# Layout of the phase products between two passes, and the order of blocks and weight loads

## The chip, the core and the metric

The kernel runs on one core of one Trainium2 chip. The metric is the device time of one execution in microseconds (us). The core's engines are PE (TensorE, matrix products; PEld is its weight load), DVE (VectorE), ACT (ScalarE), POOL (GpSimd) and SP (SyncE). SP, ACT and POOL issue DMA transfers; the transfers themselves run on 16 DMA engines. In the profile q0 is the queue of the DMAs that POOL issues, q1 that of SP, q10 that of ACT.

## The reference

The input x has 8 batches of 5696 tokens with 128 channels. The first half is a long convolution over the tokens with a filter h; its result is the x of the second half:

```python
Yf = np.fft.rfft(x, n=L, axis=1) * np.fft.rfft(h, n=L, axis=0)[None]
x = np.fft.irfft(Yf, n=L, axis=1)[:, :S, :]
theta = x @ w_theta
zr, zi = x * np.cos(theta), x * np.sin(theta)
y = np.einsum('ts,bsd->btd', w_tok_r, zr) + np.einsum('ts,bsd->btd', w_tok_i, zi)
u = x + y
out = u + np.maximum(u @ w_ch, 0.0)
```

The two products with the 5696 x 5696 matrices w_tok_r and w_tok_i (the token mixing) take most of the time.

## The kernel before, in words

*Convolution (0 to about 383 us).* The FFT is done as matrix products in 8 groups (two batches by half the channels). The result yt goes to a DRAM scratch. In the last group the phase steps of the first four batches are woven in between: `phase_step` (L736) turns a tile of 128 tokens by PE, takes sine and cosine on ACT and multiplies on DVE, which gives the two products zr and zi in one SBUF tile zz, [128, 2, 512] in bf16. It also copies the tile to a y buffer (L754; six of them in a ring) and stores it (L756).

*z's scratch and the operand blocks.* The products are the right-hand operands of the token mixing. Tokens are cut into 22 blocks a pass (p = 0, 1 are two parts of the contraction; 11 blocks j, each of four pieces i of 64 tokens). The columns are 1024, cut in two halves q (four batches each); z counts the two products. For half q = 0 of all tokens, and for what is not needed at once, `phases_b` (L550) stores 64 tokens at a time into the DRAM scratch z_hbm (L620). In SBUF a block j is a tile b{j} of 7 x 1024 columns: four operands (q, z), each with two neighbouring tokens r side by side, and three slots for sums. DVE makes five sums a block (`sum_ops`, L833; in the profile L835), since the mixing is done by seven products instead of eight (Strassen), except in the first stretches, which use the plain eight. `load_b_half` (L824) loads half q = 0 of blocks 0 to 8 for pass 0 from the scratch, by two DMAs on POOL (L829), one for each z. Half q = 1 of these blocks comes straight from zz by the home stores (L616), r = 0 on SP and r = 1 on POOL. `load_b` (L814) loads a whole block: blocks 9 and 10 of pass 0 on SP and all 11 of pass 1 on ACT, by two DMAs each (L817).

*Pass order.* The second set of 22 phase steps is woven into the first products of pass 0 (stretch i = 1, L1210): after every second product one step runs. Then pass 0 and pass 1 go through 23 token tiles each; a tile takes two chunks (6 and 5 blocks), a chunk two stretches of up to 3 blocks. L1290 is the matmul of the seven-product stretches, L1210 that of the plain ones, L1178 that of the last 64 tokens. The rest of the phase work (`bg_phase`, L911) runs beside pass 0 and stores by L623.

*W loads.* The f32 matrices come by `load_w` (L673): one load is four DMAs of 32 partitions on POOL (L680), cast to bf16, into a ring of six slots. `pump` (L652) issues loads while a slot's former chunk has been read and while their number is below ring["upto"], which the code raises by hand: six times in the last group of the convolution (`with_load`, L768), twice in stretch i = 1 (L1224), and then to the end. A chunk needs four loads. DVE transposes them (L894) before PE uses them.

*What sets the order.* Each engine runs its instructions in the program's order; a scheduler places them, but DVE's order around the start of each pass is written by hand. `tc.issue_after(...)` holds an instruction behind another on its queue. A tile that takes the place of older ones in SBUF waits until those are done with. The blocks' tiles (pool bpool_e) lie where the convolution had its own, among them yt.

Of the kernel before, what the change touches and what calls it, by code (L numbers as in the profile page):

```python
# [11 lines left out]
BF16 = mybir.dt.bfloat16  # L12
# [10 lines left out]
def kernel(  # L23
# [10 lines left out]
    nc = tc.nc  # L34
# [6 lines left out]
    BD = B * D  # L41
    HALF_PI = math.pi / 2.0

    z_hbm_h = nc.dram_tensor("z_hbm", (2, 11, 2, 2, 4, 64, BD // 2), BF16, kind="Internal")
    zl_hbm_h = nc.dram_tensor("zl_hbm", (2, 64, BD), BF16, kind="Internal")
    y2_hbm_h = nc.dram_tensor("y2_hbm", (NT, P, B, D), BF16, kind="Internal")
    wl_hbm_h = nc.dram_tensor("wl_hbm", (P, NT, P), BF16, kind="Internal")
# [502 lines left out]
    def phases_b(ti, y_ap, b0, nb, yT, sb, th_pool, th_tag, zi_eng, turns=None, tags=("red", "mag"), m=P,  # L550
                 theta_ps=None, copy=None, home={}):
        n = nb * D
        if theta_ps is None:
            theta_ps = th_pool.tile([P, n], F32, tag=th_tag, name="theta_ps")
        theta_ps = theta_ps[:m]
        y_ap = y_ap[:m]
        if tags is None:
            sin_, cos_ = (sb.tile([P, n], F16, tag=t, name=t)[:m] for t in ("sin", "cos"))
        else:
            red, mag = (sb.tile([P, n], F32, tag=t, name=t_)[:m] for t, t_ in zip(tags, ("red", "mag")))  # L560
            sin_, cos_ = (z.bitcast(F16)[:, :n] for z in (red, mag))
        if turns is None:
            for b in range(nb):
                nc.tensor.matmul(theta_ps[:, b * D:(b + 1) * D], yT[:, b, :],  # L564
                                 w_theta_sb, start=True, stop=True)
            nc.scalar.activation(red, theta_ps, AF.Identity, bias=magic[:m])  # L566
            nc.scalar.activation(mag, theta_ps, AF.Copy)
            nc.vector.scalar_tensor_tensor(red, red, MAGIC, mag,
                                           op0=ALU.subtract, op1=ALU.subtract)
            r = red  # L570
        else:
            mag = theta_ps
            ones, plus, minus, w_neg = turns
            for q in range(0, nb, 4):
                bank = theta_ps[:, q * D:(q + 4) * D]
                nc.tensor.matmul(bank, ones, plus, start=True, stop=False)
                for b in range(q, q + 4):
                    nc.tensor.matmul(theta_ps[:, b * D:(b + 1) * D], yT[:, b, :],
                                     w_theta_sb, start=False, stop=False)
                nc.tensor.matmul(bank, ones, minus, start=False, stop=False)  # L580
                for b in range(q, q + 4):
                    nc.tensor.matmul(theta_ps[:, b * D:(b + 1) * D], yT[:, b, :],
                                     w_neg, start=False, stop=(b == q + 3))
            r = theta_ps
        if copy is not None:
            copy()
        if turns is None:
            nc.scalar.activation(mag, r, AF.Abs)
        nc.scalar.activation(sin_, r, AF.Sin, bias=zero_b[:m], scale=-TWO_PI)
# [12 lines left out]
        zi_eng.tensor_mul(zi, sin_, yflat)  # L602
        nc.vector.tensor_mul(zr, cos_, yflat)
        cols = slice(b0 * D, b0 * D + n)
        q_ = b0 // 4
        for e in range((m + 63) // 64):
            rows = slice(e * 64, e * 64 + 64)
            if ti * P >= 2 * H:
                for r, z in enumerate((zr, zi)):
                    nc.sync.dma_start(zl_hbm[r, :, cols], z)  # L610
                continue
            p_, blk = divmod(2 * ti + e, 4 * NJ)
            i, j = divmod(blk, NJ)
            if tags is None and j in home:
                for r in range(2):
                    (nc.gpsimd if r else nc.sync).dma_start(  # L616
                        home[j][32 * i:32 * i + 32, :4096].rearrange("p (z q r n) -> p z q r n", z=2, q=2, r=2)[:, :, q_, r],
                        zz[e * 64 + r:e * 64 + 64:2])
            elif tags is None:
                nc.sync.dma_start(z_hbm[p_, j, q_, :, i].rearrange("z t n -> t z n"), zz[rows])  # L620
            else:
                for r, z in enumerate((zr, zi)):
                    nc.sync.dma_start(z_hbm[p_, j, q_, r, i], z[rows])  # L623

    CHUNKS = [(j0, min(CJ, NJ - j0)) for j0 in range(0, NJ, CJ)]
    pairs = (list(range(21)) + [None, 21], [0, None] + list(range(1, 22)))
# [149 lines left out]
    for g, (bp, dh) in enumerate(groups):  # L776
        st = {}
        last = g + 1 == len(groups)
        a_, load_, b_ = fronts.pop(g + 1) if g + 1 in fronts else front(g + 1)
        if last:  # L780
            for _ in range(3):
                steps0.pop(0)()
        now = ([with_load(steps0.pop(0), n < 6) for n in range(9)] if last else [], 0.0, 0.88)
        c_ = stage_c(st, last)
        if g == 0:
            ec = []
            swap_rows()
            now = ([lambda: ec.append(e_table(1)), lambda: ec.pop()(), lambda: ec.append(e_table(2)), lambda: ec.pop()(),
                    e_minus],
                   -0.1, 0.6)  # L790
        woven((c_, 0.06 if a_ else 0.0, 1.0), (a_, 0.0, 0.88), now, load_, (load_x(g + 2, st), 0.1, 1.02))
        if g == 0:
            ordered.close()
        if g + 2 == len(groups):
            xin.close()
            open_phases()
            load_ya0()
        now = [steps0.pop(0) for _ in range(5)] if last else []
        woven((b_, 0.0, 0.8), (stage_d(st, bp, dh, load_ya1 if last else None), 0.08 if b_ else 0.0, 1.1 if b_ else 1.0), now)
# [6 lines left out]
    bts_of = {0: [], 1: []}  # L806

    def tile_b(p, j, pool):
        t_ = ring["all"][:, WB:WB + BT] if j == 0 else pool.tile([P, BT], BF16, tag=f"b{j}", name=f"b{j}")
        bt = [t_[:, k * 1024:(k + 1) * 1024].rearrange("p (r n) -> p r n", r=2) for k in range(7)]  # L810
        bts_of[p].append(bt)
        return t_

    def load_b(p, j, pool, eng=nc.scalar):  # L814
        t_ = tile_b(p, j, pool)
        for z in range(2):
            sides["late"] = eng.dma_start(  # L817
                t_[:, z * 2048:(z + 1) * 2048].rearrange("p (q n) -> p q n", q=2),
                z_hbm[p, j, :, z].rearrange("q i (s r) n -> (i s) q (r n)", r=2))

    def home_pool(j):
        return bpe[0] if j < 7 else bpe[1] if j < NE else bp

    def load_b_half(j):  # L824

        t_ = home_of[j] = tile_b(0, j, home_pool(j))
        for z in range(2):
            with tc.issue_after(sides["row"]) if j else ExitStack():
                d_ = nc.gpsimd.dma_start(t_[:, z * 2048:z * 2048 + 1024],  # L829
                                         z_hbm[0, j, 0, z].rearrange("i (s r) n -> (i s) (r n)", r=2)).ins  # L830
            sides["row"] = d_ if j else sides["row"]

    def sum_ops(bt):  # L833
        b11, b12, b21, b22 = (bt[q] for q in (M2, M6, M7, M5))
# [8 lines left out]
    def sum_some(n):  # L843

        for o in [o for o in owed if o[1] <= 2 or done["used"] > o[0]][:n]:
            owed.remove(o)
            o[2]()

    for j in range(7):
        load_b_half(j)  # L850
    for step in steps0:
# [266 lines left out]
    for i, (k, p, tt, j0, s0, nj) in enumerate(stretches):  # L1118
# [97 lines left out]
        if i == 1:  # L1216
            for q, (h, s) in enumerate(((0, 0), (0, 1), (1, 0), (1, 1))):
                for n in range(4):
                    for j in range(TJ):
                        product((held, a)[s], s * TJ + j, j, n, (h,))  # L1220
                        if (n * TJ + j) % 2:
                            next_steps(1)
                    if n % 2 and q == 1:
                        ring["upto"] += 1  # L1224
                        pump()
                    if q == 3 and n == 0:
                        nxt = prepare(2)
            ring["upto"] = len(queue)
            pump()
            continue  # L1230
# [122 lines left out]
```

## Time and profile before

| what | value |
|---|---|
| median of 3 runs | 2037.92 us (2035.97 to 2045.31) |
| the profiled execution | 2040.29 us |
| its span, first to last instruction | 2038.5 us |
| mean granted PE clock | 0.987 |
| PE busy, 0 to 100 / 350 to 400 / 400 to 450 / 450 to 500 / 700 to 900 us | 74.4 / 37.1 / 47.4 / 45.2 / 198.9 us |
| PE busy, 1200 to 1300 us | 93.9 us |
| DMA queues: packets, MB, share of 16 engines | q0 322368, 157.47, 60.6%; q1 181792, 163.03, 27.3%; q10 5984, 11.54, 1.6% |
| z store (L620), 52 of 128 KB | 5.1 us to landing |
| home stores (L616), 32 on SP, 32 on POOL into b, 64 KB | 4.8 and 4.0 us |
| half block load (L829), 16 of 256 KB | 6.1 us |
| block load of pass 1 (L817 on ACT), 20 of 512 KB | 13.2 us |

How to read it: the span is the time between the first and the last instruction of one execution. A row of the timeline gives the start, the length, the engine, the line of the code, the operation, the tile written and read, and in brackets how long the engine stood idle before it and what ended that. The time to landing of a DMA runs from its issue to its completion. A wait is put down to what came last by the profile, which is inferred.

### The profile page before, as it was taken

Reading aid. Unit: us, or ns where it says so; the run is one execution under the profiler, and the core shown is the slowest. Engines: PE = TensorE matmul, PEld = TensorE weight load, DVE = VectorE, ACT = ScalarE, POOL = GpSimd, SP = SyncE. Lnnn points to the kernel's source line nnn. Section 1 sums busy time; section 2 is a strip of 40 time slices with the busy share of each in tenths; the row PEclk is TensorE's granted clock in tenths of the full one; section 3 lists DMA queues with packets and bytes.
Section 4 is the critical chain, followed back from the end, with each engine's and each line's share of the span. In section 5 each row is a group of like instructions: output and inputs, shape, how many; then the busy total and the mean of one; then the engine's idle time right before and its main releaser. Section 6 shows DMA issues by size and latency. Waiting matters only on the chain.

```text
span 2038.5 us, 42418 instructions
## 1 busy us (share of the span) xinstructions
PE 1944.0 (95%) x16121; PEld 1077.9 (53%) x16297; DVE 1539.8 (76%) x2817; ACT 638.9 (31%) x936; POOL 966.7 (47%) x1769
## 2 busy tenths in 40 slices
PE   7789898799999999999999998999999999999998
PEld 5688887654444444444444443444444444444444
DVE  8877877557778787887867668768677786777767
ACT  6788787762233323332300000111111111111111
POOL 8334213284353545454566454553545445354450
PEclk9999999899999999999999999999999999999999
DMA  9999988899798989999999798896978879788793
GB/s 155 163 173 145 161 164 231 244 261 178 157 180 173 174 173 162 181 173 181 165 173 152 122 247 206 137 154 126 153 136 141 151 126 155 130 151 142 134 157 84
DMA packets 510349, 334.77 MB, mean 164 GB/s; under 512 B 186631, under 2 KB 463111, under 8 KB 510055
## 3 DMA queue, kind: packets, MB, share of 16 engines
q0 software_dynamic: 322368, 157.47, 60.6%
q1 hardware_dynamic: 181792, 163.03, 27.3%
q10 hardware_dynamic: 5984, 11.54, 1.6%
q8 instruction: 128, 2.10, 0.4%
q14 instruction: 77, 0.63, 0.1%
HBM read 374.82 MB, written 95.24 MB: 231 GB/s over the span
## 4 chain that ended last, share of the span: by engine, by line
PE 66%; DMA 3%; DVE 3%; issue 1%; POOL 0%; ACT 0%; DVEq 0%
PE m L1290 61%; DMA ring<-in_moe_w_tok_i_dram 3%; DVE c L1297 1%; PE utp L974 1%; PE v L981 1%; PE m L1294 1%; DVE wt L894 1%; DMA ring<-in_moe_w_tok_r_dram 1%; PE theta_ps L564 0%; DVE b L835 0%; PE tpz L922 0%; PE m L1178 0%; POOL ring L680 0%; ACT ub L971 0%; DVE c L983 0%
## 5 line engine op out<-in xcount | busy, mean ns | idle before, releaser
L680 POOL DMA_DIRECT2D ring<-in_moe_w_tok_i_dram x720 | 388.6, 545 | 663.0 <-DVE wt L894 583.8
L680 POOL DMA_DIRECT2D ring<-in_moe_w_tok_r_dram x720 | 387.2, 546 | 130.2 <-DVE wt L894 70.9
L894 DVE STREAM_TRANSPOSE wt<-ring 128x384 f32<-128x384 f32 (+2 forms) x720 | 359.9, 525 | 115.6 <-PE m L1290 81.3
L1290 PE MATMUL m<-b,wt 128*128 128x512 bf16 x1604 | 384.8, 379 | 3.8 <-DVE wt L894 1.7
L1290 PEld LDWEIGHTS <-wt 128*128 128x128 bf16 x1804 | 176.0, 98 | 215.4 <-DVE wt L894 3.9
L1297 DVE TENSOR_TENSOR c<-c,m 128x512 f32<-128x512 f32 x412 | 265.9, 671 | 0.4 <-PE m L1290 0.4
L976 ACT ACTIVATE ring<-utp 128x512 bf16<-128x512 bf16 x85 | 50.7, 597 | 577.5 <-PE utp L974 577.5
L453 PE MATMUL ps<-r_u,uv_t 128*128 128x128 f16 x1024 | 117.3, 220 | 5.4 <-DVE g__1416 L460 2.0
L1210 PE MATMUL m<-b,wt 128*128 128x512 bf16 x471 | 113.0, 387 | 8.8 <-DMA b<-z_hbm 4.8
L971 ACT ACTIVATE ub<-c 128x512 bf16<-128x512 f32 x88 | 55.1, 628 | 201.0 <-DVE c L1253 118.6
L454 PE MATMUL ps<-r_v,uv_t 128*128 128x100 f16 x1024 | 115.3, 209 | 0.1
L153 POOL DMA_DIRECT2D x<-in_x_dram x128 | 99.5, 783 | 20.4 <-POOL x L151 14.9
L454 PEld LDWEIGHTS <-uv_t 128*128 128x128 f16 x1024 | 100.8, 99 | 5.9 <-issue 4.9
L433 DVE TENSOR_TENSOR uv_t<-xs,hs 128x2048 f16<-128x2048 f16 x77 | 91.5, 1223 | 16.3 <-DMA hs<-hf_hbm 9.2
L453 PEld LDWEIGHTS <-uv_t 128*128 128x128 f16 x1024 | 100.9, 98 | 2.3 <-DVE uv_t L438 2.1
L431 ACT ACTIVATE xs<-ps 128x1024 f16<-128x1024 f32 x96 | 90.8, 972 | 30.1 <-PE ps L270 14.3
L1210 PEld LDWEIGHTS <-wt 128*128 128x128 bf16 x528 | 51.5, 100 | 71.0 <-issue 12.6
L566 ACT ACTIVATE red<-theta_ps,magic 128x512 f32<-128x512 f32 (+1 forms) x46 | 31.6, 687 | 155.6 <-PE theta_ps L564 86.2
L270 PEld LDWEIGHTS <-w_t 64*128 64x128 f16 x3240 | 56.3, 98 | 31.0 <-issue 22.7
L924 ACT ACTIVATE ring<-tpz 128x512 bf16<-128x512 bf16 (+1 forms) x46 | 27.5, 597 | 134.0 <-PE tpz L922 120.2
L250 PE MATMUL ps<-f_t,x 89*128 89x180 f16 x512 | 62.0, 250 | 2.2 <-DVE a L257 1.8
L983 DVE SCALAR_TENSOR_TENSOR c<-v,c 128x512 f32<-128x512 f32 x88 | 60.1, 684 | 4.8 <-PE v L981 4.5
(2925 smaller groups left out, 3733.9 us busy)
## 6 DMA issues: line engine op xcount, KB each, us to landing
ring<-in_moe_w_tok_r_dram POOLq DMA_DIRECT2D x352, 96.0 KB, 4.4
ring<-in_moe_w_tok_i_dram POOLq DMA_DIRECT2D x352, 96.0 KB, 5.0
ring<-in_moe_w_tok_r_dram POOLq DMA_DIRECT2D x352, 80.0 KB, 4.6
ring<-in_moe_w_tok_i_dram POOLq DMA_DIRECT2D x352, 80.0 KB, 3.9
cp_hbm<-c SPq DMA_DIRECT2D x88, 256.0 KB, 2.5
c<-cp_hbm SPq DMA_DIRECT2D x88, 256.0 KB, 4.5
out_dram<-c SPq DMA_DIRECT2D x88, 256.0 KB, 4.7
hs<-hf_hbm SPq DMA_DIRECT2D x77, 256.0 KB, 3.5
```

What stands on the lines that cost most here:

```text
L153: nc.gpsimd.dma_start(x16[p0:p1, e, n0:n0 + 16, :HD], bass.AP(tensor=src.tensor, offset=src.offset + (p0 * N2 + n0) * D + dh * HD, ap=[[N2 ...
L250: nc.tensor.matmul(ps[:, i // 2, (i % 2) * 2 * K1:(i % 2 + 1) * 2 * K1], lhs(q + i), f1_t[:NB], start=True, stop=True)
L431: nc.scalar.activation(xs[:, :, :, :ck], ps, AF.Copy)
L433: nc.vector.tensor_tensor(uv[:, :, :, c0:c0 + ck], xs.rearrange("p e d k -> p e (d k)").unsqueeze(1).to_broadcast([P, 2, 2, HD * CK]), hv. ...
L453: nc.tensor.matmul(o, u_t[:, at:at + P], r_u, start=True, stop=False)
L454: nc.tensor.matmul(o[:, 2 * NP:], v_t[:, at:at + P], r_v, start=False, stop=True)
L680: nc.gpsimd.dma_start(wb[32 * i:32 * i + 32, :ng, :nj * 64], bass.AP(tensor=a.tensor, offset=a.offset + row0 * S + p * H + i * QR + j0 * 6 ...
L894: nc.vector.transpose(wt.rearrange("p j t r -> p (j t r)").bitcast(F32).rearrange("p (j g t) -> p g j t", j=TJ, g=4)[:, :ng, :nj], wb[:, : ...
L983: nc.vector.scalar_tensor_tensor(c[:m], v[:m], 0.0, c[:m], op0=ALU.max, op1=ALU.add)
L1210: nc.tensor.matmul(ms[n // 2 * 2 + h], a[n][:, j, :, r], bts_of[p][jj][n % 2 * 2 + h][:, r, :], start=(n % 2 == 0 and jj == 0 and r == 0), ...
L1290: nc.tensor.matmul(ms[q], a[q][:, j, :, r], bts[jj][q][:, r, :], start=(jj == 0 and r == 0), stop=(jj == NJ - 1 and r == 1 and q not in left))
L1297: nc.vector.tensor_tensor(c, z, ms[q], op=op)
```

## The change

1. The scratch z_hbm is laid out as (pass, block, q, piece, token, z, column) instead of (pass, block, q, z, piece, token, column): the two products of a token stand side by side. A z store from zz (L620) then has rows of 2 KB instead of 1 KB; the background stores (L623) keep rows of 1 KB, with 2 KB between them in DRAM.
2. In SBUF the four operands of a block are laid out as (q, r, z, column) instead of (z, q, r, column). A home store has one row of 2 KB a partition instead of two of 1 KB. A whole block is loaded by one DMA for each q, with rows of 4 KB, instead of one for each z with two rows of 2 KB. A half block is loaded by one DMA with rows of 4 KB instead of two with rows of 2 KB. An operand is no longer 1024 columns in a run but two runs of 512; matmuls read one run at a time, as before.
3. The tiles of blocks 0 and 6 to 1 are allocated ahead of the loads, in that order, so that they lie in SBUF the other way round. The loads of blocks 1 and 2 are no longer held behind sides["row"] (the DMAs of ya1); those from block 3 on are.
4. Of the six W loads in the last group of the convolution four stay in stage c and two move into stage d. In stretch i = 1 ring["upto"] is raised in two quarters instead of one, so four loads are issued there ahead of the rest instead of two.

```diff
-    z_hbm_h = nc.dram_tensor("z_hbm", (2, 11, 2, 2, 4, 64, BD // 2), BF16, kind="Internal")
+    z_hbm_h = nc.dram_tensor("z_hbm", (2, 11, 2, 4, 64, 2, BD // 2), BF16, kind="Internal")
...
                 for r in range(2):
+                    at = 2048 * q_ + 1024 * r
                     (nc.gpsimd if r else nc.sync).dma_start(
-                        home[j][32 * i:32 * i + 32, :4096].rearrange("p (z q r n) -> p z q r n", z=2, q=2, r=2)[:, :, q_, r],
+                        home[j][32 * i:32 * i + 32, at:at + 1024].rearrange("p (z n) -> p z n", z=2),
                         zz[e * 64 + r:e * 64 + 64:2])
             elif tags is None:
-                nc.sync.dma_start(z_hbm[p_, j, q_, :, i].rearrange("z t n -> t z n"), zz[rows])
+                nc.sync.dma_start(z_hbm[p_, j, q_, i], zz[rows])
             else:
                 for r, z in enumerate((zr, zi)):
-                    nc.sync.dma_start(z_hbm[p_, j, q_, r, i], z[rows])
+                    nc.sync.dma_start(z_hbm[p_, j, q_, i, :, r], z[rows])
...
-        now = ([with_load(steps0.pop(0), n < 6) for n in range(9)] if last else [], 0.0, 0.88)
+        now = ([with_load(steps0.pop(0), n < 4) for n in range(9)] if last else [], 0.0, 0.88)
...
-        now = [steps0.pop(0) for _ in range(5)] if last else []
+        now = [with_load(steps0.pop(0), n < 2) for n in range(5)] if last else []
...
-        bt = [t_[:, k * 1024:(k + 1) * 1024].rearrange("p (r n) -> p r n", r=2) for k in range(7)]
-        bts_of[p].append(bt)
+        raw = t_[:, :4096].rearrange("p (q r z n) -> p q z r n", q=2, r=2, z=2)
+        bt = [raw[:, k % 2, k // 2] if k < 4 else
+              t_[:, k * 1024:(k + 1) * 1024].rearrange("p (r n) -> p r n", r=2) for k in range(7)]
+        bts_of[p][j] = bt
...
-        for z in range(2):
+        for q in range(2):
             sides["late"] = eng.dma_start(
-                t_[:, z * 2048:(z + 1) * 2048].rearrange("p (q n) -> p q n", q=2),
-                z_hbm[p, j, :, z].rearrange("q i (s r) n -> (i s) q (r n)", r=2))
+                t_[:, q * 2048:(q + 1) * 2048],
+                z_hbm[p, j, q].rearrange("i (s r) z n -> (i s) (r z n)", r=2))
...
-        t_ = home_of[j] = tile_b(0, j, home_pool(j))
-        for z in range(2):
-            with tc.issue_after(sides["row"]) if j else ExitStack():
-                d_ = nc.gpsimd.dma_start(t_[:, z * 2048:z * 2048 + 1024],
-                                         z_hbm[0, j, 0, z].rearrange("i (s r) n -> (i s) (r n)", r=2)).ins
-            sides["row"] = d_ if j else sides["row"]
+        if j not in home_of:
+            home_of[j] = tile_b(0, j, home_pool(j))
+        with tc.issue_after(sides["row"]) if j > 2 else ExitStack():
+            d_ = nc.gpsimd.dma_start(home_of[j][:, :2048],
+                                     z_hbm[0, j, 0].rearrange("i (s r) z n -> (i s) (r z n)", r=2)).ins
+        sides["row"] = d_ if j > 2 else sides["row"]
...
+    for j in (0, 6, 5, 4, 3, 2, 1):
+        home_of[j] = tile_b(0, j, home_pool(j))
     for j in range(7):
         load_b_half(j)
...
-                    if n % 2 and q == 1:
+                    if n % 2 and q in (1, 2):
                         ring["upto"] += 1
                         pump()
```

More of the change, by code (lines that the diff above doesn't have):

```diff
@@ L805 @@
     bpe = [ctx.enter_context(tc.tile_pool(name="bpool_e", bufs=1, side="right", reuse_waits="tile"))]
-    bts_of = {0: [], 1: []}
+    bts_of = {0: {}, 1: {}}
     def tile_b(p, j, pool):
         t_ = ring["all"][:, WB:WB + BT] if j == 0 else pool.tile([P, BT], BF16, tag=f"b{j}", name=f"b{j}")
-        bt = [t_[:, k * 1024:(k + 1) * 1024].rearrange("p (r n) -> p r n", r=2) for k in range(7)]
-        bts_of[p].append(bt)
+        raw = t_[:, :4096].rearrange("p (q r z n) -> p q z r n", q=2, r=2, z=2)
+        bt = [raw[:, k % 2, k // 2] if k < 4 else
+              t_[:, k * 1024:(k + 1) * 1024].rearrange("p (r n) -> p r n", r=2) for k in range(7)]
+        bts_of[p][j] = bt
         return t_
```

## The prediction

> **What bounds the kernel now.** I read the page's first two parts, then PE's waits by stage, the chain, the timeline where PE waits, and the DMA queues by stretch.
>
> ```profile
> span 2038.5 us, 42418 instructions
> PE 1944.0 (95%) x16121; PEld 1077.9 (53%) x16297; DVE 1539.8 (76%) x2817; ACT 638.9 (31%) x936; POOL 966.7 (47%) x1769
> ...
> PE 66%; DMA 3%; DVE 3%; issue 1%; POOL 0%; ACT 0%; DVEq 0%
> ```
>
> PE is busy 95%, and from 520 us on it hardly waits (4 us of waits up to 1100, none over 0.2 us between 1300 and 2000). No matmul is added or removed, so only PE's idle time can change, and it lies in three places that the change touches: the phase stage (340 to 440), the first chunks of pass 0 (440 to 470), and the start of pass 1 (1180 to 1260). The first two, from the timeline (start, length, engine, line; in brackets the idle time before it and what ended it):
>
> ```profile
> 350.64 0.69 ACT L589 ACTIVATE sin<-ps,zero_b 128x512 f16<-128x512 f32 x1 [1.95 <-DVE ring L754]
> 358.79 0.42 DVE L754 COPY ring<-ps 128x512 bf16<-128x512 bf16 x1 [2.26 <-DMA y_hbm<-ring]
> 394.82 4.84 POOL L829 DMA_DIRECT2D b<-z_hbm  x9 [8.72 <-DMA y_hbm<-ring]
> 398.62 0.92 PE L1210 MATMUL m<-b,wt 128*128 128x512 bf16 x2 [3.01 <-DMA b<-z_hbm]
> 401.71 0.69 ACT L589 ACTIVATE sin<-theta_ps,zero_b 128x512 f16<-128x512 f32 x1 [4.23 <-PE theta_ps L582]
> 448.40 1.07 POOL L616 DMA_DIRECT2D b<-zz  x2
> 449.46 1.13 POOL L680 DMA_DIRECT2D ring<-in_moe_w_tok_r_dram  x2
> 454.53 5.77 PE L1210 MATMUL m<-b,wt 128*128 128x512 bf16 x25 [1.39 <-DMA b<-zz]
> 463.50 1.83 PE L1210 MATMUL m<-ring,wt 128*128 128x512 bf16 x4 [3.20 <-DVE wt L894]
> ```
>
> See: ACT paces the phase steps (0.69 + 0.59 + 0.69 = 1.97 us a step); POOL's queue stands 8.72 us before block b1 is loaded; POOL issues its last home store (zz into b) at 449, and W loads 8 and 9 come only behind it. The start of pass 1 shows in the queues between 1210 and 1215 us (packets, MB, share of 16 engines):
>
> ```profile
> q10 hardware_dynamic: 570, 1.10, 64.3%
> q0 software_dynamic: 576, 0.39, 50.6%
> ```
>
> q10 carries the block loads of pass 1 (L817), q0 the W loads. Their packets go one for one: 443 to 443 (1192-1196), 564 to 560 (1200-1205), 575 to 576, 537 to 540 (1220-1225). So how much W gets is set by how long a packet of z is.
>
> **The change, part by part.**
>
> *z stores (L620) and home stores (L616).* As many DMAs; a z store has 64 rows of 2 KB for 128 of 1 KB, a home store 32 for 64. Issue costs stay: SP takes 0.59 us for a z store of 128 rows and 0.53 to 0.59 for L623's 64, POOL 0.54 whatever the shape. What can gain is landing. In the phase steps DVE's L754 waits for a y buffer, that is for the y store six steps earlier, which stands on SP among z stores: 1.46, 0.89 and 2.26 us of DVE, which give ACT 1.95, 1.32 and 1.45 us (4.7). With packets served in turn, half as many packets land sooner. The bounds are 0 and 4.7, with nothing lost, as bytes and DMAs stay; no row shows 2 KB stores from 64 partitions. I take -2, z stores being two of the three DMAs of a step. The background stores (L623) keep 64 rows of 1 KB and now step over 2 KB in DRAM; PE does not wait for them: 0.
>
> *Blocks in reverse order, b1 and b2 not held to the ya1 DMA, one load per half block (L829).* In the changed program b1's load no longer waits for the four DMAs that read yt (issued 383.98 to 386.1; the stores land after 8.0 us); b5's does. So b1 issues at 386.1 instead of 394.8, but behind yt's 1.4 MB in the same queue, whose packets run until about 393: 0.53 MB per 2 us there puts b1 at about 396 instead of 398.5. ACT's 4.23 us stall shrinks by 2.5 (bounds 1 and 4). POOL also issues 9 DMAs fewer (9 x 0.54 = 4.9 us), 7 of them where POOL now idles.
>
> *W loads.* Of loads 4 and 5 only the last DMA each (of four) moves, from 356.6 and 362.7 into stage d; W is not needed before 440: 0. Loads 8 and 9 (8 DMAs) move ahead of the last home stores. PE's 3.20 us at 463.5 goes; what is late next is block b10, whose SP load (455.05) waits for the home stores: I keep -2.7. The price is POOL's: from load 6 to the last home store it issued 39 DMAs in 24.2 us (0.62 each), now 47, so 29.2. It starts when step 10's products are ready, 2.5 + 2 us earlier for the parts above, and no longer lags (y store 0 went out at 403.88 with its data ready at 394.7). Before, load 6 went at 425.2; now about 419, less the 2: end at 446 to 448 instead of 449.5. Behind POOL's queue wait the last home stores, for them the sums of block 8 and PE's second half of blocks 6 to 8. So of the 4.5 us gained above PE keeps only what POOL lets through: -3.5 in all at 454.5 (bounds 0 and -6), the -2 and the -2.5 included. The y-slot stall on DVE (2.19 us at 439.96, then PE 2.04) goes into the same wait.
>
> *Sums (L835).* 110 of 128x1024 now read and write 512-element runs with gaps, at 684 ns before. Nearest row: L433, three-level operands, 128x2048 in 1222 ns, so 0.60 ns an element against 0.67. Cost 0; the upper bound is a rival below.
>
> *Pass 1 loads (L817).* 22 DMAs of 512 KB, rows of 4 KB for 2 KB. PE's waits for late blocks (1.08 + 0.72 us at 1248 and 1251) go: -1.8. Against that stands W. A pair of packets took 16 x 5 / 573 = 140 ns of an engine; by bytes read (1.93 KB of z, about 1.3 KB of f32 W) a pair with 3.86 KB takes 223. A W load came every 5.2 us in this stretch (POOL's issues, which wait for landings), so 8.1 us while z runs. The fifth one after 1190.5, W22 of the first chunk of pass 1, landed at about 1218.1 and PE needs it transposed at 1223.2, 4.5 us of slack. At 8.1 it is 10 us late. Bounds: 0 (a 4 KB row takes two turns, and the ratio stays) and +10; the nearest row is yt's, whose 5.6 KB rows show as single packets (66 of 0.32 MB at 388 to 390), so nearer the upper end. Less a part: z now outruns PE's release of blocks (b3 at about 1200, b6 at 1209) and leaves W gaps. I take +6.
>
> [...]
>
> **Sum.** -3.5 - 2.7 - 1.8 + 6 = -2.0 us. The profiled execution took 2040.3 (span 2038.5); that gives 2038.3. The median of the runs shown is 2037.9, 2.4 below that execution, so 2036 on its scale. Bounds: all gains (-6, -3.2, -1.8) and no starvation -11; no gain and all loss +10.
>
> **Rivals.**
> 1. *Faster, about 2027*: W keeps its share, or its delay hides in the slack, and POOL's queue keeps up. -6 - 3.2 - 1.8 = -11. For it: POOL issues at 0.56 when its queue is full (433.8 to 449.5, 28 DMAs), which ends it 3 us sooner. Against: the one-for-one counts.
> 2. *Slower, about 2044*: starvation of W at the start of pass 1. +10, less 1.8, with only 2 of the early gains passing POOL: +6. Break-even against the forecast's early 6.2 + 1.8: W 8 us late, that is W loads 7.7 us apart instead of 5.2; beyond that the change loses. For it: the counts and the shares; against: z runs out of released blocks.
> 3. *Sums at half speed, about 2060*: 1.07 + 0.1 us instead of 0.68 is +0.5 x 110 = 55 us of DVE, at 454 to 511 and 1215 to 1270; DVE idles some 14 us of the first stretch, so PE would lose 10 to 14 in each. Against: L433. [...]
> 4. *It does not do what it says*: b1 still held (by a z store, or PE), POOL's new W loads eat the rest: 2038.
>
> **How the numbers follow.** Forecast (2030 to 2041) 0.50; rival 1 0.25; rival 2 0.16; rival 3 0.03; rival 4 0.06. Range 2024 to 2046: it takes in rivals 1 and 2 and leaves their tails and rival 3 out. 0.5% (10 us, about what a measurement can tell from no change) is 2027.7 and 2048.1: faster 0.20 (most of rival 1), slower 0.09 (rival 3, the tail of 2), same 0.71.
>
> **What would show it.** Right: POOL's first L829 of b1 near 386; PE's wait for b1 1 us or less; W loads 8 and 9 before the last home store, which goes out at 446 to 448; no wait at 463; between 1192 and 1230 q0 and q10 equal in packets at some 360 each per 5 us, and a wait of PE for a W transpose near 1220. Wrong: q0's packets as many as before there; L835 over 0.8 us; POOL's last home store after 450; a PE wait for W between 470 and 1180.

## The result, and the profile after

The changed kernel takes 2049.48 us (median of 12 runs, 2043.29 to 2053.80), the kernel before 2038.53 (12 runs, 2030.50 to 2045.31); the ratio is 1.0049, 95% interval [1.0033, 1.0064]. The change costs about 10 us. The forecast was 2036, with a range up to 2046. In the changed kernel lines from load_b on have numbers larger by 5 or less (W loads L680 to L681, transposes L894 to L899, sums L835 to L838, home stores L616 to L617, half loads L829 to L832, stretch i = 1 L1210 to L1215).

The page of the changed kernel (span; busy time of the engines; the chain that ended last):

```profile
span 2042.6 us, 42399 instructions
PE 1941.3 (95%) x16121; PEld 1074.6 (53%) x16297; DVE 1537.9 (75%) x2817; ACT 638.3 (31%) x936; POOL 959.0 (47%) x1760
PE 55%; DVE 4%; DMA 3%; issue 2%; POOL 1%; ACT 0%; DVEq 0%
```

PE does the same work in the same busy time (16121 matmuls, 1941.3 us busy against 1944.0). The loss is idle time of PE, and PE's timeline has it in the places that the prediction read (start, length, engine, line; in brackets the idle time before it and what ended it). First the start of pass 1 in the kernel before, then the changed kernel:

```profile
1248.42 1.89 PE L1210 MATMUL m<-b,wt 128*128 128x512 bf16 x8 [1.08 <-DMA b<-z_hbm]
1251.03 1.02 PE L1210 MATMUL m<-b,wt 128*128 128x512 bf16 x4 [0.72 <-DMA b<-z_hbm]
1259.77 0.61 PE L974 MATMUL utp<-ident_bf,ub 128*128 128x128 bf16 x4 [3.41 <-ACT ub L971]
```

```profile
391.62 0.82 PE L1215 MATMUL m<-b,wt 128*128 128x512 bf16 x2 [2.49 <-DMA b<-z_hbm]
404.11 0.38 PE L750 MATMUL tpz<-ident_bf,ya 128*128 128x128 bf16 x4 [2.38 <-DVE ring L755]
453.08 7.11 PE L1215 MATMUL m<-b,wt 128*128 128x512 bf16 x23 [6.97 <-DMA b<-zz]
461.91 1.04 PE L1215 MATMUL m<-ring,wt 128*128 128x512 bf16 x4 [1.29 <-DVE wt L899]
1223.93 1.18 PE L1215 MATMUL m<-ring,wt 128*128 128x512 bf16 x4 [4.54 <-DVE wt L899]
1264.40 0.61 PE L979 MATMUL utp<-ident_bf,ub 128*128 128x128 bf16 x4 [6.04 <-ACT ub L976]
```

See: the wait for the last home store (b<-zz) went from 1.39 to 6.97 us, though the prediction had it shrink; the wait for W behind it fell from 3.20 to 1.29. At the start of pass 1 there is a wait of 4.54 us for a W transpose that was not there before, and the wait for ub (the tile that ACT copies from the accumulations c) at the end of that token tile grew from 3.41 to 6.04. In the phase stage the wait for b1 fell from 3.01 to 2.49 us only, and 2.38 us behind a y copy (404.11) are new.

Why the wait for ub grew too is on DVE's timeline. First the kernel before, then the changed one: the transposes of W between 1206 and 1250 us ahead of which DVE stood more than 0.7 us.

```profile
1228.35 0.58 DVE L894 STREAM_TRANSPOSE wt<-ring 128x384 f32<-128x384 f32 x1 [1.55 <-DMA ring<-in_moe_w_tok_i_dram]
1234.51 0.58 DVE L894 STREAM_TRANSPOSE wt<-ring 128x384 f32<-128x384 f32 x1 [0.79 <-DMA ring<-in_moe_w_tok_r_dram]
1240.43 0.58 DVE L894 STREAM_TRANSPOSE wt<-ring 128x384 f32<-128x384 f32 x1 [2.96 <-DMA ring<-in_moe_w_tok_i_dram]
```

```profile
1206.78 0.58 DVE L899 STREAM_TRANSPOSE wt<-ring 128x384 f32<-128x384 f32 x1 [0.73 <-DMA ring<-in_moe_w_tok_i_dram]
1214.59 0.58 DVE L899 STREAM_TRANSPOSE wt<-ring 128x384 f32<-128x384 f32 x1 [0.95 <-DMA ring<-in_moe_w_tok_r_dram]
1223.30 1.50 DVE L899 STREAM_TRANSPOSE wt<-ring 128x384 f32<-128x384 f32 x3 [6.96 <-DMA ring<-in_moe_w_tok_i_dram]
1232.11 0.58 DVE L899 STREAM_TRANSPOSE wt<-ring 128x384 f32<-128x384 f32 x1 [0.97 <-DMA ring<-in_moe_w_tok_r_dram]
1236.91 0.58 DVE L899 STREAM_TRANSPOSE wt<-ring 128x384 f32<-128x384 f32 x1 [4.23 <-PE m L1215]
```

See: DVE stood 5.3 us before and 13.8 after, 8.5 us more. 4.3 of these are for W loads (9.6 against 5.3); the last wait, 4.23 us, ends with PE, which is late by then. In these stretches DVE has transposes, sums and accumulations in an order written by hand with hardly a gap besides these (none above 0.3 us between 1214 and 1265 us in either kernel), so what it loses to a late W load comes back at the end of the tile, where the accumulations, and behind them ub, stand behind the sums. PE shows only a part of the loss at the place where W is late.

One trap in comparing the two traces: the program ahead of the first phase step is the same in both, yet that step comes at 334.0 us before and at 329.0 after (between 328.2 and 338.6 in the profiles of this study). Five microseconds of luck hide more than half of the loss in the profiled execution (2044.42 us). So the traces are compared by fixed instructions, counted from the first phase step's sine on ACT. Difference to the kernel before, in us (positive is later); the four columns are the last phase step's sine, the first accumulation of pass 0 (549.4 us before), an accumulation after the start of pass 1 (1307.3), and the last one:

| kernel | phase steps | pass 0 | pass 1 begun | end |
|---|---|---|---|---|
| changed kernel | +0.6 | +1.0 | +9.1 | +9.2 |
| 2 KB rows | -1.5 | -2.1 | -3.8 | -3.8 |
| two early W loads | -0.5 | -5.8 | +2.5 | +2.5 |
| both | -1.7 | -8.6 | -6.4 | -6.5 |
| order alone, old layout | +2.1 | +2.0 | +3.9 | +3.9 |
| 1 KB rows | +1.7 | -0.4 | +3.2 | +3.1 |
| both, eight small DMAs at the program's start | -0.3 | -3.1 | -3.3 | -3.3 |
| both, old order and old W loads | -2.5 | -2.9 | -3.0 | -3.1 |
| both, 4 KB rows for blocks 6 to 10 | -0.6 | -6.2 | -1.5 | -1.4 |
| both, eight small DMAs in place | -1.8 | -2.9 | -1.5 | -1.5 |
| 2 KB rows, late y stores on SP | +1.7 | -3.3 | -3.1 | -3.1 |
| both, late y stores on SP | +0.2 | -7.7 | -7.2 | -7.2 |

These are single executions: "both" and the row with small DMAs at the program's start run the same program from 51 us on and differ by 5.5 us at the second mark. What a row gains or loses from the second mark to the third is steadier, and sorts the kernels by the rows of pass 1: 4 KB +8.0 and +8.3, 4 KB for the late blocks alone +4.8, 1 KB +3.6, 2 KB -1.7 to +2.2. From the third mark to the end no kernel gains or loses more than 0.1 us against the kernel before.

### The profile page after: what moved, and what is told of

Its sections match the earlier page's. It is cut to its first block, busy times and chain, and to the rows that moved or that the text cites. A ratio compares the mean times of both kernels' runs of the same rounds, so it can differ in the third digit from the quotient of the medians.

```text
span 2042.6 us, 42399 instructions
## 1 busy us (share of the span) xinstructions
PE 1941.3 (95%) x16121; PEld 1074.6 (53%) x16297; DVE 1537.9 (75%) x2817; ACT 638.3 (31%) x936; POOL 959.0 (47%) x1760
## 4 chain that ended last, share of the span: by engine, by line
PE 55%; DVE 4%; DMA 3%; issue 2%; POOL 1%; ACT 0%; DVEq 0%
PE m L1295 51%; DMA ring<-in_moe_w_tok_i_dram 2%; DVE c L1302 1%; POOL ring L681 1%; PE utp L979 1%; PE v L986 1%; PE m L1299 1%; DVE wt L899 1%; DVE b L838 1%; DMA ring<-in_moe_w_tok_r_dram 1%; PE m L1183 1%; PE theta_ps L564 0%; PE tpz L927 0%; DMA wl<-in_moe_w_tok_r_dram 0%; DMA wl<-in_moe_w_tok_i_dram 0%
## 5 line engine op out<-in xcount | busy, mean ns | idle before, releaser
L681 POOL DMA_DIRECT2D ring<-in_moe_w_tok_i_dram x720 | 388.1, 546 | 669.9 <-DVE wt L899 585.6
L899 DVE STREAM_TRANSPOSE wt<-ring 128x384 f32<-128x384 f32 (+2 forms) x720 | 359.8, 524 | 122.7 <-PE m L1295 77.6
L681 POOL DMA_DIRECT2D ring<-in_moe_w_tok_r_dram x720 | 386.7, 547 | 138.2 <-DVE wt L899 77.5
L1215 PE MATMUL m<-b,wt 128*128 128x512 bf16 x471 | 114.0, 389 | 12.1 <-DMA b<-zz 7.4
L433 DVE TENSOR_TENSOR uv_t<-xs,hs 128x2048 f16<-128x2048 f16 x77 | 91.5, 1224 | 13.7 <-ACT xs L431 7.9
L1215 PEld LDWEIGHTS <-wt 128*128 128x128 bf16 x528 | 51.1, 100 | 77.8 <-issue 16.2
```

What stands on the lines that cost most here:

```text
L433: nc.vector.tensor_tensor(uv[:, :, :, c0:c0 + ck], xs.rearrange("p e d k -> p e (d k)").unsqueeze(1).to_broadcast([P, 2, 2, HD * CK]), hv. ...
L681: nc.gpsimd.dma_start(wb[32 * i:32 * i + 32, :ng, :nj * 64], bass.AP(tensor=a.tensor, offset=a.offset + row0 * S + p * H + i * QR + j0 * 6 ...
L899: nc.vector.transpose(wt.rearrange("p j t r -> p (j t r)").bitcast(F32).rearrange("p (j g t) -> p g j t", j=TJ, g=4)[:, :ng, :nj], wb[:, : ...
L1215: nc.tensor.matmul(ms[n // 2 * 2 + h], a[n][:, j, :, r], bts_of[p][jj][n % 2 * 2 + h][:, r, :], start=(n % 2 == 0 and jj == 0 and r == 0), ...
```

## The experiments

In the ratios each kernel stands against runs of the kernel before on the same chip.

**Pass 1, rows of 2 KB.** The changed kernel, but:

```diff
             sides["late"] = eng.dma_start(
+                t_[:, :4096].rearrange("p (q r m) -> p q r m", q=2, r=2)[:, :, q],
+                z_hbm[p, j].rearrange("q i (s r) z n -> (i s) q r (z n)", r=2)[:, :, q]) if p else eng.dma_start(
                 t_[:, q * 2048:(q + 1) * 2048],
                 z_hbm[p, j, q].rearrange("i (s r) z n -> (i s) (r z n)", r=2))
```

> The changed kernel with one edit: the block loads of pass 1 have rows of 2 KB again (two DMAs a block, one for each of the two tokens r, instead of one for each half q), everything else as in the change. Theory (W starved by the longer packets of z at the start of pass 1): between 1192 and 1215 us q0 and q10 move some 560 packets each per 5 us again instead of 385, PE's wait of 4.5 us for a W transpose near 1224 is gone, and the time falls by the 8.9 us that pass 1 lost from 1180 to 1310, to about 2041. Rival (the loss comes from the layout itself: a block's first product now needs both of its DMAs, or split operands slow PE and DVE): the wait and the time stay, about 2049.

Measured: 2039.16 us, ratio 1.0002 [0.9988, 1.0016]. PE's wait near 1224 is gone, DVE's waits for W are near those of the kernel before, and the loss of pass 1 is gone with them:

```profile
1227.93 0.58 DVE L901 STREAM_TRANSPOSE wt<-ring 128x384 f32<-128x384 f32 x1 [0.91 <-DMA ring<-in_moe_w_tok_i_dram]
1234.28 0.58 DVE L901 STREAM_TRANSPOSE wt<-ring 128x384 f32<-128x384 f32 x1 [0.98 <-DMA ring<-in_moe_w_tok_r_dram]
1240.19 0.58 DVE L901 STREAM_TRANSPOSE wt<-ring 128x384 f32<-128x384 f32 x1 [2.95 <-DMA ring<-in_moe_w_tok_i_dram]
```

The theory held: .0047 of the ratio, 9.6 us, hang on the rows, with the layout, the sums and the number of DMAs unchanged; the marks in the table have 9.7 for the start of pass 1 (-1.7 against +8.0). One more thing differs: a DMA now carries one token r of both halves and not one half q, so a block's first product needs both of its DMAs, which would work against the gain.

**Pass 1, rows of 1 KB.** Four DMAs a block, one for each half q and product z:

```diff
...
+            for z in range(2):
+                sides["late"] = eng.dma_start(
+                    t_[:, q * 2048:(q + 1) * 2048].rearrange("p (m z n) -> p m z n", m=2, z=2)[:, :, z],
+                    z_hbm[p, j, q].rearrange("i (s r) z n -> (i s) r z n", r=2)[:, :, z])
```

> The changed kernel with one edit: the block loads of pass 1 have rows of 1 KB (four DMAs a block). Theory (queues take turns by packet, so the length of a z row sets W's share): one-for-one counts again, at some 800 packets each per 5 us between 1195 and 1215 (a pair is 98 ns, the 140 ns of 2 KB rows less half of the 83 ns that the 4 KB rows added); W is never late, but z moves 0.8 MB per 5 us instead of 1.1, its loads end 10 us or more later than with 2 KB rows, and PE waits 3 to 12 us for blocks around 1230 to 1260; the time lies between that with 2 KB rows (2039) and 2050. Rival (rows matter by efficiency, not by turns): counts are not equal, W's bytes per 5 us are as with 2 KB rows, and the time is within 2 us of 2039.

Measured: 2045.21 us (10 runs), ratio 1.0037 [1.0022, 1.0053]. The queues between 1205 and 1210 us (packets, MB, share of 16 engines), first of the changed kernel, then with 2 KB rows, then with 1 KB rows:

```profile
q10 hardware_dynamic: 390, 1.43, 76.7%
q0 software_dynamic: 386, 0.27, 34.4%
```

```profile
q10 hardware_dynamic: 575, 1.11, 64.8%
q0 software_dynamic: 575, 0.39, 50.6%
```

```profile
q0 software_dynamic: 766, 0.52, 67.4%
q10 hardware_dynamic: 762, 0.74, 53.3%
```

Read the first number of each pair: equal at every row length in these 5 us, to 4 packets. Elsewhere the counts part: with 1 KB rows 567 and 1008 between 1200 and 1205, in the changed kernel 270 on q10 and 482 on q0 between 1220 and 1225, and 13 and 938 between 1235 and 1240, when the last block load had long been issued (1229.0). That one queue is short of work wherever they part is the author's reading. In the 5 us shown the rows of z that ACT asks for decide how many rows of W get through: 0.27, 0.39 and 0.52 MB, while z goes the other way with 1.43, 1.11 and 0.74. An estimate from the counts, with all 16 engines taken as full: one pair takes 16 engines x 5 us / 388 = 206 ns of an engine, then 139 ns and 105 ns. With 4 KB rows PE waits for W, with 1 KB rows for z (here, with 1 KB rows):

```profile
1254.66 0.38 PE L1221 MATMUL m<-b,wt 128*128 128x512 bf16 x1 [1.77 <-DMA b<-z_hbm]
1258.99 0.59 PE L1221 MATMUL m<-b,wt 128*128 128x512 bf16 x1 [3.95 <-DMA b<-z_hbm]
```

The theory held. 2 KB is the best of the three (1.0002, against 1.0049 with 4 KB and 1.0037 with 1 KB): both are then nearly in time, with DVE's waits for W at 0.91, 0.98 and 2.95 us there (shown above) and PE's waits for blocks of pass 1 at 2.6, 0.8 and 1.8 us in the kernel with both edits, below.

**Rows of 4 KB for the late blocks only.** Does W's urgency end with the first blocks? "Both" (2 KB rows and two early W loads, below) with rows of 4 KB for blocks 6 to 10:

```diff
-                z_hbm[p, j].rearrange(...)[:, :, q]) if p else eng.dma_start(
+                z_hbm[p, j].rearrange(...)[:, :, q]) if p and j < 6 else eng.dma_start(
```

> The version with 2 KB rows and two early W loads (2031.8), with rows of 4 KB for blocks 6 to 10 of pass 1 (one DMA for each half). Theory (turns by packet: 2 KB rows leave W its share while W is urgent, longer rows bring the late blocks sooner): PE's waits for blocks of pass 1 (2.6 + 0.8 + 1.8 us) shrink to under 2 us in sum and no wait for W of over 1 us comes; 2028 to 2030. Rival (W is as urgent then): a wait for a W transpose of 2 us or more between 1225 and 1260, time 2033 or more.

Measured: 2039.16 us, ratio 1.0019 [1.0004, 1.0034], against 0.9970 without the edit. The rival held: no wait for a block of 0.3 us or more is left, but

```profile
1244.07 6.22 PE L1217 MATMUL m<-b,wt 128*128 128x512 bf16 x27 [2.79 <-DVE wt L901]
1262.77 0.61 PE L981 MATMUL utp<-ident_bf,ub 128*128 128x128 bf16 x4 [6.04 <-ACT ub L978]
```

W is as urgent then as at first: DVE stands 3.77, 3.23 and 4.16 us for W loads between 1224 and 1244, and the wait for ub follows. The size is less sure than the sign: the runs have .0049 (10 us), the one profile of each kernel 5 us at the last mark.

**Two early W loads.** The changed kernel, but:

```diff
-                    if n % 2 and q in (1, 2):
+                    if n % 2 and q == 1:
```

> The changed kernel with one edit undone: in stretch i = 1 two W loads instead of four are issued ahead of the rest. Theory (W loads 8 and 9 in POOL's queue push back the last home stores): POOL's last home store goes out some 4 to 6 us earlier than the 449.9 us of the change, PE's wait of 7.0 us at 453 falls to 1 to 3 us, and a wait of 3 us or more for W near 460 comes back in place of 1.3; the time changes by -2 (bounds -5 and +1), to about 2047. Rival (POOL is held back by landings of its own queue, not by the number of instructions): the 7.0 us stay and the time is the same or longer.

Measured: 2042.57 us, ratio 1.0016 [1.0000, 1.0033]. The sign was right and the size too small: .0033, 6.7 us. PE has no wait of 0.4 us or more for a home store, and one of 2.52 us for W at 452.6; POOL's last home store ends at 438.6. The first phase step comes at 329.0 us in both kernels, so the two times can be set side by side: 438.6 here, 449.95 in the changed kernel, 11.3 us apart and not the 4 to 6 expected.

**Both edits.** 2 KB rows and two early W loads:

> Both edits of the two runs before at once. Theory: the effects add, as they lie 700 us apart: 8.9 + 2 us below the change, about 2039, the same as the kernel before. Rival (layout costs by itself): 2047 or more.

Measured: 2031.77 us (6 runs), ratio 0.9970 [0.9959, 0.9982]. The effects add: from the four ratios, row length is worth .0047 with four early W loads and .0046 with two, and the early W loads .0033 with 4 KB rows and .0032 with 2 KB. This is 6 us faster than the kernel before and 16 us faster than the changed kernel; the expectation of no gain was too low, since the rest of the change gains.

**The order edits alone.** The kernel before, with blocks in reverse, b1 and b2 not held, four W loads in stage c and two in stage d, and four early W loads; layout and rows as before:

```diff
-            with tc.issue_after(sides["row"]) if j else ExitStack():
+            with tc.issue_after(sides["row"]) if j > 2 else ExitStack():
...
+    for j in (0, 6, 5, 4, 3, 2, 1):
+        home_of[j] = tile_b(0, j, home_pool(j))
...
-                    if n % 2 and q == 1:
+                    if n % 2 and q in (1, 2):
```

> The kernel before with the order edits alone: reversed blocks, b1 and b2 not held, four W loads in stage c and two in stage d, four raised early in stretch i = 1; layout and rows as before, so two DMAs of 1 KB pieces a home store row and two half loads a block. Theory (starvation by 4 KB rows): pass 1 starts as in the kernel before, without a wait for W near 1224; the early part is as in the change, 1 to 4 us worse than before; about 2041. Rival (the W loads moved in the change shift the ring and make pass 1 late): 2047 or more, with the wait near 1224.

Measured: 2043.30 us, ratio 1.0030 [1.0016, 1.0044]: 6 us slower, more than the 1 to 4 expected, and about what the early W loads cost elsewhere. PE waits 7.39 us for a home store (at 461.4). At the start of pass 1 PE's waits for W are at most 0.7 us, though DVE stands 7.9 us for W loads there against 5.3 before; one profile does not tell whether that is the order's doing.

**The layout without the order edits.** With 2 KB rows in pass 1, the blocks in the old order, b1 and b2 held, and W loads as in the kernel before:

```diff
-        with tc.issue_after(sides["row"]) if j > 2 else ExitStack():
+        with tc.issue_after(sides["row"]) if j else ExitStack():
...
-    for j in (0, 6, 5, 4, 3, 2, 1):
-        home_of[j] = tile_b(0, j, home_pool(j))
...
-                    if n % 2 and q in (1, 2):
+                    if n % 2 and q == 1:
```

> The layout alone, with 2 KB rows in pass 1: scratch and SBUF layout as in the change, one load a half block, but blocks in the old order, b1 and b2 held, and W loads as in the kernel before. It tells how much of the early gain of the version with 2 KB rows and two early W loads (2031.8) comes from the layout and how much from the block order. Theory (stores with 2 KB rows land sooner, POOL issues fewer DMAs): 3 us gained by 372 us, 5 us or more by 549, time 2032 to 2035. Rival (the release of b1 and b2 is what gains): time as the kernel before, 2036 to 2039, with POOL idle 8 us or more before b1 and PE's wait for b1 at 3 us.

Measured: 2033.45 us, ratio 0.9973 [0.9960, 0.9987]. The layout with 2 KB rows gains by itself (5.5 us); the order edits without the early W loads add nothing that can be told from zero (0.9970). PE waits 4.29 us for b1 here and 2.92 in "both", but 1.68 to 4.13 in all the kernels with the new order, so the profiles do not show what the release of b1 is worth by itself. What they suggest is a loss right behind it: from 386 us to the last phase step this kernel falls back by 1.1 us against the kernel before, and those with the new order and y stores on POOL by 1.5 to 4.5.

**W loads 8 and 9: issue or bytes?** Into "both" went eight DMAs of 256 bytes on POOL, at first without an order:

```diff
+                    if n % 2 and q == 2:
+                        for x in range(4):
+                            nc.gpsimd.dma_start(tiny_h.ap()[...], moe_w_tok_r[x:x + 1, :64])
```

> The version with 2 KB rows and two early W loads (2031.8), with eight extra DMAs of 256 bytes on POOL's queue, at the two places in stretch i = 1 where the change issues W loads 8 and 9; they move a scrap of W into a scratch that nobody reads. They have the issue cost of those loads without their bytes. Theory (W loads 8 and 9 cost by POOL's issue, 8 x 0.55 = 4.4 us): POOL's last home store goes out 4.4 us later, PE's wait for it grows from 1.1 to some 5 us, and the time is some 4 us longer, 2036. Rival (they cost by their bytes and rows, which home stores and y stores of the same queue stand behind): last home store under 1.5 us later than without them, time within 1.5 us of 2032.

Measured: 2032.12 us, ratio 0.9969 [0.9953, 0.9986]. This says nothing about the question: the trace has the eight between 4.6 and 51 us, as they depend on nothing and the scheduler put them first. It repeats "both" with 12 runs. Then each was held behind the last home store issued so far:

```diff
+                            with tc.issue_after(sides["home"].ins):
```

> The version with 2 KB rows and two early W loads (2031.8), with eight extra DMAs of 256 bytes on POOL's queue in the very places where the change has W loads 8 and 9 (four behind the home stores of step 16, four ahead of the last two); in the run of this before, the scheduler had put them at the start of the program, so it was a repeat of 2031.8. They move a scrap of W into a scratch that nobody reads. Theory (W loads 8 and 9 cost by POOL's issue, 8 x 0.55 = 4.4 us): POOL's last home store goes out 4 us or more later than in the version without them, PE's wait for it grows from 1.1 to some 5 us, time 2036. Rival (they cost by their bytes and rows, behind which home stores and y stores stand in the same queue): last home store under 2 us later, time within 1.5 us of 2032.

Measured: 2033.85 us, ratio 0.9999 [0.9983, 1.0014], so .0029 or 6 us more than "both", near the .0032 of the W loads themselves (each ratio has an interval of .0015 or so to either side). POOL of this kernel:

```profile
430.15 1.98 POOL L1237 DMA_DIRECT2D tiny_hbm<-in_moe_w_tok_r_dram  x4
432.11 0.58 POOL L758 DMA_DIRECT2D y_hbm<-ring  x1
432.69 1.15 POOL L618 DMA_DIRECT2D b<-zz  x2
434.69 0.58 POOL L758 DMA_DIRECT2D y_hbm<-ring  x1 [0.86 <-DMA tiny_hbm<-in_moe_w_tok_r_dram]
...
436.86 1.94 POOL L1237 DMA_DIRECT2D tiny_hbm<-in_moe_w_tok_r_dram  x4
438.79 0.58 POOL L758 DMA_DIRECT2D y_hbm<-ring  x1
439.37 1.03 POOL L618 DMA_DIRECT2D b<-zz  x2
440.41 0.58 POOL L758 DMA_DIRECT2D y_hbm<-ring  x1
442.40 0.52 POOL L618 DMA_DIRECT2D b<-zz  x1 [1.42 <-DMA tiny_hbm<-in_moe_w_tok_r_dram]
443.45 0.51 POOL L618 DMA_DIRECT2D b<-zz  x1 [0.53 <-DMA tiny_hbm<-in_moe_w_tok_r_dram]
```

The eight cost 1.98 + 1.94 us of issue, and 0.86 + 1.42 + 0.53 us in which POOL stands until a DMA has landed: 6.7 us together. What it waits for can be read from the semaphores in the traces. POOL's DMAs tell of their landing by eight semaphores in turn (99 to 106, 210 DMAs on each in the kernel before), and an issue waits until the DMA eight places ahead of it has landed: in all thirteen traces, wherever that landing is recorded, no issue on POOL comes less than 0.27 us after it, and never are more than seven other POOL DMAs in flight. The three waits here end 0.28 to 0.54 us after the landing of the eighth DMA ahead, two of them after that of a small one, issued 5.0 and 5.8 us earlier than it landed. The last home store ends 12.4 us after the last phase step's sine, in "both" 5.9 and 8.3 us (the two profiles). PE's wait for a home store is 4.17 us instead of 1.09 and 3.27. So the number of DMAs on POOL's queue, with hardly a byte in them, accounts for most of the cost, by the middle of the intervals for nearly all of it. POOL of the changed kernel shows the same form with real W loads:

```profile
434.22 2.22 POOL L681 DMA_DIRECT2D ring<-in_moe_w_tok_r_dram  x4
...
440.85 2.21 POOL L681 DMA_DIRECT2D ring<-in_moe_w_tok_i_dram  x4
...
443.62 0.56 POOL L617 DMA_DIRECT2D b<-zz  x1
445.28 0.52 POOL L617 DMA_DIRECT2D b<-zz  x1 [1.11 <-DMA y_hbm<-ring]
447.51 0.57 POOL L757 DMA_DIRECT2D y_hbm<-ring  x1 [1.72 <-DMA b<-zz]
448.92 1.03 POOL L617 DMA_DIRECT2D b<-zz  x2 [0.83 <-DMA ring<-in_moe_w_tok_i_dram]
```

2.22 + 2.21 us of issue, then 1.11 + 1.72 + 0.83 us of waits for landings, each ended 0.28 to 0.54 us after the eighth DMA ahead had landed. The size of these waits varies from execution to execution: the kernel with 1 KB rows, the same program up to pass 1, has POOL's load 6 and its last home store 27.2 us apart, the changed kernel 32.9 and the one with 2 KB rows 32.2.

**Relief for POOL.** The y stores of the last ten phase steps go on SP, in the kernel with 2 KB rows and four early W loads, and in "both":

```diff
+            late_ = hh and len(steps1) < 10
-                (nc.gpsimd if hh else nc.sync).dma_start(
+                (nc.gpsimd if hh and not late_ else nc.sync).dma_start(
```

> The changed kernel with 2 KB rows in pass 1 (2039), W loads 8 and 9 early as in the change, and the y stores of the last ten phase steps on SP instead of POOL. Theory (POOL's queue is what the early W loads overfill): POOL issues 10 DMAs fewer there (5.7 us), PE's wait of 6.7 us for the last home store falls to 2 us or less, time 2034. Rival (q0's bytes, or SP becomes the limit of the phase steps): the wait stays above 4 us or ACT stalls for y slots, time 2037 or more.

Measured: 2040.29 us, ratio 1.0025 [1.0008, 1.0042], against 1.0002 without the edit. The wait for a home store went (0.96 us is left), as the theory said, but the time did not fall: a wait of 3.39 us for W at 462.2 took its place, a y copy holds PE 2.51 us at 410.6 (1.98 without the edit), and the last phase step is 3.2 us later than without the edit.

> The version with 2 KB rows and two early W loads (2031.8), with the y stores of the last ten phase steps on SP instead of POOL. Theory: POOL is no longer what the last home store waits for, but PE's waits there are 1.1 and 1.3 us by now, so at most 2 us come of it: 2030 to 2032. Rival (SP becomes the limit of the phase steps): 2034 or more.

Measured: 2033.15 us, ratio 0.9997 [0.9982, 1.0011]. By the runs the edit costs 5 us, by the one profile nothing (-7.2 against -6.5 at the end). SP may be the next limit, in the steps that now have their y store there too; no run tests that, and why the runs and the profile differ stays open.

## Why the prediction was wrong

**Pass 1: right mechanism, size too small, and it decides.** The prediction foresaw equal packet counts at some 360 per 5 us (390 and 386), a pair of 223 ns (206), W loads 8.1 us apart (POOL's first issues of three loads in a row at 1201.7, 1209.1 and 1217.2: 7.4 and 8.1), and a wait for a W transpose near 1220 (1223.93). What failed is the step "I take +6", and the discount behind it, "z now outruns PE's release of blocks": q10 kept its 385 to 390 packets per 5 us until 1210. The gain of 1.8 us on late blocks did come (no wait for a block of 0.3 us or more is left in pass 1, though PE came late to these blocks anyway), and still pass 1 as a whole lost 8.0 us between the marks, 9.6 by the undo, where the forecast had +6 - 1.8 = +4.2. So the W term, mis-sized at +6, was 8 to 9.6 us, or 9.8 to 11.4 if the gain on the blocks is counted as earned: about its upper bound of 10. (The 8.1 us between W loads are a slip, 5.2 x 223 / 140 is 8.3; nothing hangs on it.) The working error was to price the lateness against the slack of PE's first use of one load (W22, 4.5 us). The engine to price it on was DVE: between 1214 and 1265 us of the changed kernel it has no gap above 0.5 us but the waits for W and the one for PE shown above, so a load that comes late is idle time of DVE. The three runs with 1, 2 and 4 KB rows agree with turns whose length is set by the rows (766 and 762, 575 and 575, 386 and 390 packets in the same 5 us); the turns themselves stand in no trace.

**W loads 8 and 9: wrong sign.** The step was "PE keeps only what POOL lets through: -3.5 in all at 454.5" and -2.7 at 463. It had POOL's load 6 go out at about 417, 47 DMAs at 0.62 us (29.2 us) from there, and the last home store out at 446 to 448. Measured on the same scale (5.0 us added, since the first phase step came that much earlier): load 6 at 422.1, 32.9 us for the 47 DMAs, the last home store at 455.0. So three things were wrong. The start was 5 us late, because the gain of 4.5 us in the phase steps that was to bring it forward was not there (+0.6 at the last step; see below). POOL does not only issue: it stands until the eighth DMA ahead has landed, 3.7 us in the three waits shown. And the comparison was with the wrong end: the last home store of the kernel before (449.5) was set against 446 to 448, while the change without the early W loads has it out at 438.6 by the clock of the changed kernel, 11.3 us ahead of the 449.95 measured with them. So the early loads cost all of this lead, and not the little by which the queue was to be late. The step at 463 was of the right kind (3.20 to 1.29) but worth 1.9 and not 2.7. All in all the early W loads cost 6.6 us (mean of .0033 and .0032) and were booked as a gain.

**What held.** The z and y stores: -2 forecast up to 372 us; -1.6 in the changed kernel and -2.8 to -3.6 in the others with its layout, -0.7 with the order alone. The y stores on SP land after 6.0 us, 7.6 before. The half load of b1 went out where it was forecast (379.5, which is 386.1 with the 5.0 us of the first step and the 1.6 gained by then). The sums on split operands take 684 ns, as before: rival 3 is out. Its 1.07 + 0.1 us, for which it names no row, is near an estimate from two rows of the kernel before: L433 takes 1223 ns for 2048 elements and L438 687 for 1024, so twice the 536 ns between them is 1.07 us, and 0.15 us stands besides. Rival 4 is out too, as b1 was released.

**The release of b1: -2.5 that was not there.** The load issued at 379.5 landed 12.1 us later: yt's stores were issued ahead of it on the same queue, at 378.5 and 379.0, as the prediction said, and landed after 9.2 and 11.0 us where it had 8.0. PE's wait for b1 is 2.49 us, and ACT's stall went from 4.23 to 3.69, so the term is -0.5. Then comes what the prediction did not have: the first y and home stores that POOL issued behind the half loads land 8 to 10 us after their issue, DVE's y copy stands 2.61 us for a y buffer (403.63), and PE (2.38) and ACT (2.61 us at 405.41) stand behind it. At the last phase step the changed kernel is 0.6 us later than the kernel before, where the prediction had it 4.5 us earlier.

**Which case it was.** Rival 2 (2044) has the right place, sign and mechanism. It had the starvation at its full +10, but let 2 us of the early gains through, where the early part of the change costs about 1 us. By the runs the account closes: the layout -5.5, the early W loads +6.6, the 4 KB rows +9.6 make +10.7, where 10.0 (.0049) were measured.

## What to carry to other kernels

A longer DMA row is not a gain in itself: here z's rows of 4 KB left W 0.27 MB in 5 us, where rows of 2 KB left it 0.39, and the kernel lost 9.6 us. Where two queues have work at once, find out which of the two is later, price its lateness on the engine without slack (here DVE and not PE), and try the size between. Loads moved ahead on an engine that issues a full queue can delay what stands behind them even with hardly a byte in them: here eight DMAs of 256 bytes had POOL's last home store out 12.4 us after the last phase step's sine, against 5.9 and 8.3 without them. Count the DMAs, and look how many the program lets be in flight (eight on POOL here, beyond which it stood 2.8 us for landings). And take a compound change apart: here the layout gains 5.5 us, the row length in one place loses 9.6 and two early loads 6.6, and the sum hides the gain.

## What was not expected of the hardware

Eight DMAs of 256 bytes held POOL 2.8 us beyond their issue time of 3.9 us: they move almost nothing, but the two that POOL waited for land as late as the large ones around them (5.0 and 5.8 us after issue), and until it lands each keeps one of the eight semaphores. That limit is in this program's semaphores; no run shows how many DMAs the queue itself would take. Issue on SP became cheaper with fewer rows, where the prediction has "Issue costs stay": a z store of 64 rows takes 472 ns where one of 128 rows took 592 (medians of 52), a home store 544 for 601 (32), while POOL's went from 544 to 522 only.
